# Attention with a dense layer behind it: one softmax for both heads of the 64-row first tile, and a new order of steps

## Chip, cores, metric

One Trainium2 chip, one of its cores. The metric is device time in microseconds (us) of one execution. Engines: PE multiplies matrices, DVE and POOL work elementwise on vectors, ACT applies functions and copies, SP issues most transfers.

## What is computed

```python
B, H, S, D = 4, 8, 576, 64                      # q, k, v: [B, H, S, D]
scores = q @ k.T / sqrt(D), causal              # per head, S x S
a = softmax(scores);  local = a @ v
phi = where(q > 0, q, exp(q) - 1) + 1
mem = (phi @ M_prev) / (phi @ z_prev + 1e-6)
attn = g * mem + (1 - g) * local                # g = sigmoid(beta) of the head
x = attn as [B*S, H*D]                          # [2304, 512]
r = relu(x @ w_in)                              # [2304, 2048]
out = (s * r * r + b) @ w_out                   # [2304, 512]
```

## The kernel before

The 32 heads are taken two at a time, in 16 pairs (`attention(g)`, four pairs for each of the four batch rows). The 576 rows of a head are cut into five tiles of queries: tile 0 with 64 rows, tiles 1 to 4 with 128. Tile 0 is loaded twice, on partitions 0 to 63 and 64 to 127. Buffers of a pair alternate (`u = g % 2`).

For a pair the steps are: load q and k transposed (`load_qk`, L340), q in rows (L291) and z (L292); the feature map of q (`phi`, ACT L295 and L300, DVE L301, products with z L305, normalisers on DVE L307 to L311, writes into P L318); score matmuls on PE in three visits (`scores`, L370 in fp32 for pairs 0 to 7; L364 for pairs 8 to 15, as three fp32r products of a high and a low half that `split` makes, L396 and L398). DVE adds the mask and takes the minimum of each row (`red`, L377), ACT takes the exponential and its sum (`ex`, L383), DVE inverts the sums (L440, L441), POOL or DVE scales the rows (`scale`, L389). PE transposes P in four banks (`bank`, L468), ACT or DVE copies them from PSUM (`copy`, L477 to L484), and `second` (L520) multiplies by V and M. The result is split into a high and a low fp32r half (L541, L542) as `xs`. Weights `w_in` are converted in 20 pieces (`convert`, L564 to L579). The first matrix product (`mm1`, L586 to L588) takes a batch row at a time, in groups of 12 matmuls, two halves of 6 (`first`); what is left of it runs after the attention, with PSUM tiles named hps, beside the preparation of `w_out`. The second product (L866 to L870, yps) is last.

The steps of the attention and the groups of `first` are given to a planner (`Plan.add`) with an engine, a cost and what they read and write. `Plan.deal(ORDER)` puts the steps of each engine in the order of a long table of numbers and merges the engines by modelled starts; so ORDER fixes what stands in a row on every engine, and each engine works through its row in order. `Plan.waits` finds waits of PE in that model and fills them with matmuls of no use (`warm`, L247). Letters choose engines by pair: RELU, ZMUL, PUTS (writes into P), COPY (banks), SCAL (scalings), HIGH and LOW (halves of weights), QL (low halves of q and k); HOME chooses the PSUM pool of a group.

In tile 0 the softmax ran per head on all 128 partitions, so each row was worked twice; the fourth bank (k = 3) took tile 0 from partitions 64 to 127 alone, and had 4 transposes in one PSUM tile and 6 in the other.

## Time and profile before

| | us |
|---|---|
| median of 3 runs (539.62 to 540.48) | 539.95 |
| the profiled execution | 540.74 |
| its span, first to last instruction | 538.9 |
| PE busy in the span | 529.4 |
| ACT busy | 408.1 |
| DVE busy | 406.8 |
| POOL busy | 276.4 |
| first row of the rest of the first product (tile hps) starts at | 270.96 |

The busy time of PE is 98% of the span, and the granted clock is full in every slice. These are sums over stages: in the first tenth of the run ACT and DVE are busy almost without a break, later PE is. So the reader should take each stage by itself.

### The profile page before, as it was taken

The page shows a single profiled execution, that of the slowest core. Times are in us where ns is not written, and L with a number is a line of the kernel's source. Part 1 is how long each engine was busy: PE and PEld are TensorE (multiplying, and loading weights), DVE is VectorE, ACT ScalarE, POOL GpSimd, SP SyncE. Part 2 cuts the span into 40 slices and gives each one's busy share as a digit, 9 for nine tenths or more (in the row PEclk, how much of TensorE's full clock was granted, in tenths as well). Part 3 has the DMA queues.
Part 4 walks back from the last instruction along what each step waited for, and adds up shares of the span by engine and source line. Part 5 has one row for each costly group of instructions (what it writes and reads, how often), then busy time and mean ns, then how long its engine had stood idle before and what let it go on. Part 6 is the DMA issues. An engine that isn't in the chain of part 4 may idle for free.

```text
span 538.9 us, 11602 instructions
## 1 busy us (share of the span) xinstructions
PE 529.4 (98%) x4158; PEld 444.4 (82%) x4158; DVE 406.8 (75%) x986; ACT 408.1 (76%) x898; POOL 276.4 (51%) x275
## 2 busy tenths in 40 slices
PE   8989999999999999999999999999999999999997
PEld 6767777777878778877788888899999998999996
DVE  5999998998877958334169796435798889889873
ACT  6999999889987637547346679769987887897840
POOL 4999557663784623022100001407768768768760
PEclk9999999999999999999999999999999999999999
DMA  7666667755243621121294746356354353452101
GB/s 223 183 178 193 227 219 253 227 155 196 89 150 101 223 84 59 61 79 44 90 376 165 267 174 219 128 192 204 110 161 121 115 167 114 129 174 89 40 30 40
DMA packets 56666, 81.51 MB, mean 151 GB/s; under 512 B 7584, under 2 KB 39072, under 8 KB 56608
## 3 DMA queue, kind: packets, MB, share of 16 engines
q1 hardware_dynamic: 54064, 78.63, 44.8%
q10 hardware_dynamic: 2544, 2.14, 1.2%
q8 instruction: 33, 0.54, 0.4%
q14 instruction: 25, 0.20, 0.1%
HBM read 57.15 MB, written 23.59 MB: 150 GB/s over the span
## 4 chain that ended last, share of the span: by engine, by line
PE 90%; ACT 6%; DVE 2%; issue 1%; DMA 1%; ACTq 0%; DVEq 0%
PE yps L866 12%; PE yps L870 11%; PE sb L520 7%; PE tb L586 7%; PE tb L587 6%; PE tb L588 6%; PE hps L586 5%; PE hps L587 5%; PE hps L588 5%; PE yps L869 5%; PE yps L868 5%; PE tb L468 4%; PE sb L364 4%; ACT P L383 3%; PE sb L370 2%; PE sb L586 1%
## 5 line engine op out<-in xcount | busy, mean ns | idle before, releaser
L389 POOL TENSOR_SCALAR P<-P,sr,omg 128x448 f32<-128x448 f32 (+4 forms) x120 | 89.2, 758 | 37.0 <-DVE sr L441 26.3
L870 PE MATMUL yps<-rb,op 128*128 128x256 f32 x360 | 101.1, 281 | 0.0
L383 ACT ACTIVATE P<-P,mn 128x448 f32<-128x448 f32 (+4 forms) x160 | 90.0, 568 | 9.6 <-DVE mn L377 9.3
L377 DVE CUSTOM_DVE_ANT_0 P<-sb,mask 128x320 f32<-128x320 f32 (+4 forms) x160 | 72.6, 480 | 24.4 <-PE sb L364 21.8
L866 PE MATMUL yps<-rb,op 128*128 128x512 f32 x216 | 76.9, 396 | 0.0
L870 PEld LDWEIGHTS yps<-rb,op 128*128 128x128 f32 x360 | 67.9, 189 | 0.0
L846 POOL TENSOR_TENSOR sum<-src 128x512 f32<-128x512 f32 x10 | 13.0, 1298 | 91.2 <-ACT src L830 76.6
L854 POOL TENSOR_TENSOR op<-src,op 128x512 fp32r<-128x512 f32 x30 | 43.9, 1484 | 20.2 <-ACT op L853 20.1
L877 DVE TENSOR_TENSOR yu<-yu,yps 128x256 f32<-128x256 f32 x90 | 36.5, 414 | 20.0 <-PE yps L870 19.0
L866 PEld LDWEIGHTS yps<-rb,op 128*128 128x128 f32 x216 | 40.6, 188 | 9.0
L468 PEld LDWEIGHTS tb<-ident,P 64*128 64x128 f32 x928 | 35.9, 139 | 9.6 <-issue 4.3
L468 PE MATMUL tb<-ident,P 64*128 64x64 f32 x928 | 40.9, 226 | 2.2 <-DVE xs L542 0.7
L868 PE MATMUL yps<-rb,op 128*128 128x256 f32 x144 | 40.5, 281 | 0.0
L869 PE MATMUL yps<-rb,op 128*128 128x256 f32 x144 | 40.5, 281 | 0.0
L853 ACT CAST op<-src 128x512 fp32r<-128x512 f32 x50 | 30.5, 615 | 12.0 <-PE yps L870 9.6
L854 DVE TENSOR_TENSOR op<-sum,op 128x512 fp32r<-128x512 f32 x36 | 38.7, 1075 | 0.3 <-ACT op L853 0.2
L593 ACT ACTIVATE r<-hps 128x256 f32<-128x256 f32 x62 | 21.8, 385 | 19.4 <-DMA r_d<-r 14.4
L854 POOL TENSOR_TENSOR op<-w1H,op 128x512 fp32r<-128x512 f32 x24 | 35.0, 1489 | 0.0
L318 POOL TENSOR_TENSOR P<-qs,nrm 128x384 f32<-128x384 f32 (+1 forms) x24 | 18.8, 797 | 31.5 <-DVE nrm L311 23.0
L586 PE MATMUL tb<-xs,w0H 128*128 128x512 f32 x80 | 32.9, 412 | 0.0
L383 ACT ACTIVATION_READ_ACCUMULATOR P<-P,mn 128x1 f32 x160 | 32.3, 202 | 0.0
L370 PE MATMUL sb<-qk 64*128 64x288 f32 (+4 forms) x192 | 30.3, 411 | 1.9 <-DVE mn L377 1.7
(177 smaller groups left out, 1618.5 us busy)
## 6 DMA issues: line engine op xcount, KB each, us to landing
r_d<-r SPq DMA_DIRECT2D x41, 256.0 KB, 2.3
src<-r_d SPq DMA_DIRECT2D x20, 512.0 KB, 4.4
qk<-in_qk_t_dram SPq DMA_DIRECT2D x15, 576.0 KB, 5.0
raw<-in_moe_w_out_dram SPq DMA_DIRECT2D x16, 512.0 KB, 6.2
w1H<-r_d SPq DMA_DIRECT2D x16, 512.0 KB, 4.7
xa<-in_moe_w_in_dram SPq DMA_DIRECT2D x12, 512.0 KB, 4.8
r_d<-r SPq DMA_DIRECT2D x48, 128.0 KB, 1.9
qs<-in_q_rows_dram SPq DMA_DIRECT2D x16, 320.0 KB, 3.2
```

The costliest lines, as they stand in the source:

```text
L377: nc.vector.tensor_tensor_reduce(P[:, j, PB[i] + 64:PB[i] + 64 + n], at(ps, j, o, n), m, -SCALE, 3.0e38, ALU.add, ALU.min, mn[:, j, i:i + 1])
L383: nc.scalar.activation(pt, pt, AF.Exp, scale=-1.0, bias=mn[:, j, i:i + 1], accum_out=sm[:, j, i, 0:1])
L389: e.tensor_scalar(pt, pt, sr[:, j, i:i + 1], omg[:, h:h + 1], ALU.mult, ALU.mult)
L468: nc.tensor.transpose(TB[ps[h]][:, o[h]:o[h] + 64], P[rs, j, c:c + 128], ident[rs, rs], tile_position=(64 * h, 0))
L586: nc.tensor.matmul(ps, lhsT=wH[:, p, fs], rhs=xs[:, 0], start=p == 0, stop=False)
L587: nc.tensor.matmul(ps, lhsT=wH[:, p, fs], rhs=xs[:, 1], start=False, stop=False)
L588: nc.tensor.matmul(ps, lhsT=wL[:, p, fs], rhs=xs[:, 0], start=False, stop=p == NP - 1)
L854: (nc.gpsimd if m in ONPOOL else nc.vector).tensor_sub(L, x, H.bitcast(F32))
L866: nc.tensor.matmul(tile, lhsT=H, rhs=B, start=f == 0, stop=False)
L868: nc.tensor.matmul(ps, lhsT=H, rhs=B[:, 0], start=f == 0, stop=False)
L869: nc.tensor.matmul(ps, lhsT=H, rhs=B[:, 1], start=False, stop=False)
L870: nc.tensor.matmul(ps, lhsT=L, rhs=B[:, 0], start=False, stop=f == KF - 1)
```

## The change

For tile 0 the two heads now share one set of 128 partitions: head 0 keeps rows on partitions 0 to 63, head 1 on 64 to 127. `red` stays two instructions of 64 partitions each, writing into one place; `ex` and `scale` are one instruction each. A small write (`put01`) brings head 1's feature map of tile 0 into that place, `open_gates` makes a column of gates (OM) that has head 0's gate above and head 1's below, and the fourth bank has five transposes in each of its PSUM tiles, copied in two pieces. Pairs 8 to 15 score tile 0 in fp32 straight from q and k, so `split` skips the first 128 columns. `Plan.waits` may fill a wait from the time when a PSUM tile comes free in it, and with one matmul too. The letters, modelled costs of transfers, HOME and the table ORDER are new; the counts of steps differ by what is named above.

```diff
@@ Plan.waits
-            n = int((b["start"] - a["end"] - 0.4) / cost)
-            free = [(pool, k) for pool in pools for k, held in enumerate(self.held[pool])
-                    if all(z <= a["end"] or y >= b["start"] for y, z in held)]
-            if n > 1 and free:
-                more.append(dict(start=a["end"], fn=lambda n=n, at=free[0]: fn(n, *at)))
+            free = []
+            for pool in pools:
+                for k, held in enumerate(self.held[pool]):
+                    if all(y >= b["start"] or z < b["start"] for y, z in held):
+                        free.append((max([a["end"]] + [z + self.LAT for y, z in held if a["end"] < z < b["start"]]), pool, k))
...
+            n = int((b["start"] - t - 0.4) / cost)
+            if n > 0:
@@ setup
         warm(WARM, TB[3])
+        nc.tensor.matmul(TB[3][:, :64], lhsT=busy, rhs=busy[:, :64], start=True, stop=True)
@@ letters (PUTS, HIGH and LOW shown of eight)
-    PUTS = "DDPPDPPDPPPPPPPP"
-    HIGH, LOW = "PPAPAAPPAAAAAAAAAAPA", "PDPDDPPDDDPDPDDDDDDD"
+    PUTS = "PDPPDPPDPPPPPDPP"
+    HIGH, LOW = "APAAAAPAAAAAAAAAAAAP", "PDPDDPDPDDPPDDDDDDDD"
@@ phi
+        def put01():
+            put(384, 768, slice(1, None, -1))
+            o = P[64:128, 0, PB[0]:PB[0] + 64]
+            vec.tensor_mul(o, q[64:128, 0, 1], n[64:128, 0, 1].to_broadcast([64, 64]))
@@ scores
-                if fast:
+                if fast and i:
@@ red
+            if i == 0:
+                rs = slice(64 * j, 64 * j + 64)
+                nc.vector.tensor_tensor_reduce(
+                    P[rs, 0, PB[0] + 64:PB[0] + 128], at(ps, j, o, n)[rs], mask[rs, 576:640], -SCALE, 3.0e38, ALU.add, ALU.min, mn[rs, 0, 0:1])
+                return
@@ scale
-            e.tensor_scalar(pt, pt, sr[:, j, i:i + 1], omg[:, h:h + 1], ALU.mult, ALU.mult)
+            e.tensor_scalar(pt, pt, sr[:, j, i:i + 1], omg[:, h:h + 1] if i else OM[:, p:p + 1], ALU.mult, ALU.mult)
@@ split of pairs 8 to 15
-            for k, (a, z) in enumerate(((QF, QF + S), (0, QF))):
+            for k, (a, z) in enumerate(((QF, QF + S), (128, QF))):
@@ the exponentials and the scalings
-                    add("ACT", EXP[i], lambda i=i, j=j: ex(i, j), r + 0.15 + 0.01 * k, [("mn", u, i, j)],
-                        [("p", u, i, j), ("sm", u, i, j)])
+                    if i or j:
+                        add("ACT", EXP[i], lambda i=i, j=j * (i > 0): ex(i, j), r + 0.15 + 0.01 * k, [("mn", u, i, h) for h in ((j,) if i else range(2))],
+                            [("p", u, i, j), ("sm", u, i, j)] + [("p", u, 0, 0), ("sm", u, 0, 0)] * (i == 0))
-                for j in range(2):
+                for j in heads(i):
@@ bank
-            o = [0, 0]
+            o = [64, 64] if k == 3 else [0, 0]
-                        if i == 0 and h == 0:
+                        if i == 0:
+                            if h == j:
+                                nc.tensor.transpose(
+                                    TB[ps[h]][:, 0:64], P[rs, 0, c:c + 128], ident[rs, rs], tile_position=(64 * h, 0))
                             continue
@@ copy, k = 3
-            elif h:
-                put(F[:, :, 0:384].rearrange("p j (r c) -> p j r c", c=128)[:, :, :, 0:64],
-                    t[:, 0:384].rearrange("p (j r c) -> p j r c", j=2, c=64))
             else:
-                put(half(F[:, :, 64:320]), t[:, 0:256].rearrange("p (j r c) -> p j r c", j=2, c=64))
+                put(half(F[:, :, 64:320]), t[:, 64:320].rearrange("p (j r c) -> p j r c", j=2, c=64))
+                put(F[:, h, 0:64], t[:, 0:64])
@@ gates
+    def open_gates():
+        for j in range(2):
+            nc.gpsimd.tensor_copy(OM[64 * j:64 * j + 64], omg.rearrange("r (p j) -> r p j", j=2)[64 * j:64 * j + 64, :, j])
@@ ORDER, first numbers of the table
-        0, 1, 5, 50, 11, 14, 16, 32, 2, 4, 7, 3, 6, 8, 30, 33, 36, 40, 53, 76, 81, 87, 84, 13, 18, 20, 21, 25, 19, 23, 24, 28, 39, 42, 66, 62, 54, 52, 22, 27,
+        0, 3, 5, 95, 13, 19, 21, 27, 29, 1, 4, 9, 2, 6, 7, 22, 26, 35, 40, 55, 63, 72, 90, 79, 12, 17, 18, 30, 15, 38, 23, 36, 42, 43, 51, 54, 62, 16, 24, 32,
```

On ACT, the end of the fourth pair (g = 3; pt and F are the copies of its banks, w0H the rounding of a weight piece, P an exponential). Before:

```order
L477 COPY pt<-tb_100 128x8x64
L477 COPY pt<-tb_101 128x8x64
L479 COPY F_125<-tb_99 128x2x4x64
L479 COPY F_125<-tb_98 128x2x4x64
L484 COPY F_125<-tb_100 128x2x2x64
L481 COPY F_125<-tb_101 128x2x3x64
L566 ACTIVATE xa<-xa 128x256
```

After:

```order
L500 COPY pt<-tb_100 128x8x64
L500 COPY pt<-tb_98 128x8x64
L502 COPY F_126<-tb_101 128x2x4x64
L502 COPY F_126<-tb_99 128x2x4x64
L504 COPY F_126<-tb_100 128x2x2x64
L505 COPY F_126<-tb_100 128x64
L504 COPY F_126<-tb_98 128x2x2x64
L505 COPY F_126<-tb_98 128x64
L401 ACTIVATE P_121,sm_117<-P_121,mn_115 128x192
```

The copies of 128x2x3x64 and 128x2x2x64 became two of 128x2x2x64 and two of 128x64.

On SP, the first transfers of the program (qk_106, qs_110 and z_108 belong to the first pair, qk_107, qs_111 and z_109 to the second). Before:

```order
L340 DMA qk_106<-in_qk_t_dram 128x2x192
L340 DMA qk_106<-in_qk_t_dram 128x2x256
L291 DMA qs_110<-in_q_rows_dram 128x640
L340 DMA qk_106<-in_qk_t_dram 128x2x128
L292 DMA z_108<-in_z_prev_dram 128x128
L340 DMA qk_107<-in_qk_t_dram 128x1152
```

After:

```order
L353 DMA qk_106<-in_qk_t_dram 128x2x192
L353 DMA qk_106<-in_qk_t_dram 128x2x256
L299 DMA qs_110<-in_q_rows_dram 128x640
L300 DMA z_108<-in_z_prev_dram 128x128
L300 DMA z_109<-in_z_prev_dram 128x128
L353 DMA qk_106<-in_qk_t_dram 128x2x128
L353 DMA qk_107<-in_qk_t_dram 128x1152
```

Both z loads moved ahead of the last piece of the first pair's q and k.

On PE, a visit of scores of a pair from 8 on (x6 counts three products for each of two heads). Before:

```order
L364 MATMUL sb_97<-qks 128x448 x6
L364 MATMUL sb_97<-qks 128x64 x6
L364 MATMUL sb_97<-qks 128x320 x6
L364 MATMUL sb_97<-qks 128x192 x6
```

After:

```order
L377 MATMUL sb_96<-qks 128x448 x6
L383 MATMUL sb_96<-qk_106 128x64 x2
L377 MATMUL sb_97<-qks 128x320 x6
L377 MATMUL sb_97<-qks 128x192 x6
```

The six products of 64 columns became two, read from qk.

## Rows read from the trace of the kernel before

**Rows 1.** Windows: length; busy us of PE, PEld, DVE, ACT, POOL; granted clock; DMA

```profile
7.50:53.40 45.90, 42.70 (x492) 31.88 (x490) 44.59 (x173) 45.87 (x136) 41.12 (x55) 1.00 0.66 202
...
56.60:271.00 214.40, 213.51 (x1920) 166.08 (x1917) 153.84 (x472) 160.29 (x421) 102.29 (x118) 1.00 0.43 139
```

**Rows 2.** Waits of PE from 56 to 272: who ended them, us, times, longest

```profile
PE tb L468 <- DVE nrm L311: 0.6, 1, 0.6
PE sb L520 <- DVE mn L377: 0.3, 1, 0.3
```

**Rows 3.** The chain of waits, 0 to 60: start, us, what

```profile
52.67 0.64 ACT F L481
53.36 3.35 PE tb L520 x32
```

**Rows 4.** Timeline of ACT, 38.7 to 53.5: start, us, instruction

```profile
39.46 0.56 ACT L481 COPY F<-tb 128x384 f32<-128x384 f32 x1
39.83 0.46 ACT L484 COPY F<-tb 128x256 f32<-128x256 f32 x1
40.10 0.50 ACT L575 CAST w0H<-xa 128x256 fp32r<-128x256 f32 x1
40.40 0.44 ACT L383 ACTIVATE P<-P,mn 128x64 f32<-128x64 f32 x1
...
40.75 0.64 ACT L383 ACTIVATE P<-P,mn 128x320 f32<-128x320 f32 x1
...
47.63 0.29 ACT L541 CAST x<-tb 128x64 fp32r<-128x64 f32 x1
47.73 0.47 ACT L541 CAST xs<-tb 128x256 fp32r<-128x256 f32 x1
```

**Rows 5.** Groups by shape on DVE, 0 to 53.4: busy us, mean ns

```profile
L318 DVE TENSOR_TENSOR P<-qs,nrm 128x384 f32<-128x384 f32 x2 | 1.3, 648 | 0.0
```

**Rows 6.** Groups by shape on PE, 56 to 271

```profile
L364 PE MATMUL sb<-qks 64*128 64x64 f32 x48 | 3.5, 244 | 0.0
L370 PE MATMUL sb<-qk 64*128 64x64 f32 x8 | 0.7, 244 | 0.0
```

**Rows 7.** Timeline of PE, 52 to 58, the first product's start

```profile
56.64 0.50 PE L586 MATMUL tb<-xs,w0H 128*128 128x512 f32 x1
56.98 0.39 PE L587 MATMUL tb<-xs,w0H 128*128 128x512 f32 x1
57.21 0.39 PE L588 MATMUL tb<-xs,w0L 128*128 128x512 f32 x1
```

**Rows 8.** Transfers issued from 0 to 4: count, size each, us from issue to landing

```profile
qk<-in_qk_t_dram SPq DMA_DIRECT2D x1, 128.0 KB, 4.4
z<-in_z_prev_dram SPq DMA_DIRECT2D x1, 64.0 KB, 5.7
```

**Rows 9.** Timeline of all engines, 0 to 14

```profile
2.74 0.55 SPq L340 DMA_DIRECT2D qk<-in_qk_t_dram  x1
3.34 0.60 SPq L292 DMA_DIRECT2D z<-in_z_prev_dram  x1
...
8.61 1.57 PE L370 MATMUL sb<-qk 64*128 64x288 f32 x8
...
10.21 0.76 DVE L377 CUSTOM_DVE_ANT_0 P<-sb,mask 128x576 f32<-128x576 f32 x1
```

**Rows 10.** Transfers issued from 23 to 25

```profile
xa<-in_moe_w_in_dram SPq DMA_DIRECT2D x1, 256.0 KB, 2.8
z<-in_z_prev_dram SPq DMA_DIRECT2D x1, 64.0 KB, 2.9
```

**Rows 11.** Windows: busy us of each engine, 56 to 80

```profile
56.00:80.00 24.00, 24.00 (x170) 19.02 (x166) 23.60 (x78) 23.57 (x62) 13.11 (x15) 1.00 0.65 212
```

**Rows 12.** Timeline of PE, 65 to 67 and 85 to 90: bursts of scores

```profile
65.03 1.24 PE L370 MATMUL sb<-qk 64*128 64x288 f32 x8
...
85.49 1.48 PE L370 MATMUL sb<-qk 64*128 64x288 f32 x8
```

More of the change, by code (lines that the diff above doesn't have):

```diff
@@ L132, in waits @@
         for a, b in zip(pe, pe[1:]):
-            n = int((b["start"] - a["end"] - 0.4) / cost)
-            free = [(pool, k) for pool in pools for k, held in enumerate(self.held[pool])
-                    if all(z <= a["end"] or y >= b["start"] for y, z in held)]
-            if n > 1 and free:
-                more.append(dict(start=a["end"], fn=lambda n=n, at=free[0]: fn(n, *at)))
+            free = []
[3 more added lines that the diff above has]
+                        free.append((max([a["end"]] + [z + self.LAT for y, z in held if a["end"] < z < b["start"]]), pool, k))
+            if not free:
+                continue
+            t, pool, k = min(free, key=lambda x: x[0])
+            n = int((b["start"] - t - 0.4) / cost)
+            if n > 0:
+                more.append(dict(start=a["end"], fn=lambda n=n, pool=pool, k=k: fn(n, pool, k)))
         return more
@@ L231, in attention_moe_kernel @@
     NRM = two([128, 5, 2, 1], "nrm")
+    OM = ap1.tile([128, NP], F32, name="om")
     MN, SM, SR = two([128, 2, 5], "mn"), two([128, 2, 5, 2], "sm"), two([128, 2, 5], "sr")
@@ L345, in attention @@
         for v, (a, z) in enumerate(chunks):
-            add("SP", 0.9 if a == 0 and g else 0.5, lambda a=a, z=z: load_qk(a, z), (r0 if g else 0) - 4.0 + 0.01 * v, writes=[("qk", u, v)],
-                bytes=128 * 8 * (z - a) + 32768 * (a == 0 and g > 0))
+            add("SP", 0.9 if g else 0.6, lambda a=a, z=z: load_qk(a, z), (r0 if g else 0) - 4.0 + 0.01 * v, writes=[("qk", u, v)],
+                bytes=(400000, 190000, 200000)[v] if g == 0 else 380000 if g == 1 else 128 * 8 * (z - a) + 32768, slack=2 if g else 1)
         if g == 0:
@@ L413, in attention @@
             if fast:
-                cost = sum(n + 32 for _, _, n, _ in group) / 800 + 0.05
+                cost = sum(max(107, (n + 32) / 2.4 + 2) for i, _, n, _ in group if i) * 0.003 + (0.22 if v == 0 else 0.05)
             add("PE", cost, lambda group=group, ps=ps: scores(group, ps), r,
-                [(x, u, k) for x in ("qh", "ql") for k in range(2)] if fast else [("qk", u, k) for k in range((1, 2, 2, 3)[v] if g == 0 else 1)] + [("qk", 0, "d")] * (g == 0),
+                [(x, u, k) for x in ("qh", "ql") for k in range(2)] + [("qk", u, 0)] * (v == 0) if fast else [("qk", u, k) for k in range((1, 2, 2, 3)[v] if g == 0 else 1)] + [("qk", 0, "d")] * (g == 0),
                 [("sc", g, v), "visit"], take=[(ps, "S")] * (2 if v == len(visits) - 1 else 1), mode="row")
@@ L422, in attention @@
                     take=[(free, "T")], give=[(free, 0, "T")], mode="row")
+            heads = lambda i: range(2) if i else range(1)
             tiles = [(i, o - c0) for i, c0, n, o in group if c0 + n == QW[i]]
@@ L434, in attention @@
                 continue
-            keys = [("sm", u, i, j) for i in mine for j in range(2)]
-            inv = [("sr", u, i, j) for i in mine for j in range(2)]
+            keys = [("sm", u, i, j) for i in mine for j in heads(i)]
+            inv = [("sr", u, i, j) for i in mine for j in heads(i)]
             low = sorted(mine)
@@ L492, in attention @@
             PS.update({k: [] for k in ks})
-            add("PE", sum(0.11 + 0.11 * len(BANKS[k]) - (k == 3) * 0.06 for k in ks), lambda ks=ks: [bank(k, PS[k]) for k in ks], r,
+            add("PE", sum(0.11 + 0.11 * len(BANKS[k]) - (k == 3) * 0.12 for k in ks), lambda ks=ks: [bank(k, PS[k]) for k in ks], r,
                 [("p", u, i, j) for i in tiles for j in range(2)] + [("phi", u, i) for k in ks for kt, i in BANKS[k] if kt == 0]
@@ L500, in attention @@
             for h in range(2):
[L501 removed]
+                cost = dict(A=0.48 if k < 3 else 0.36, D=0.58 if k < 3 else 0.45)
                 c = COPY[g][k]
```

32 lines of the change are left out of this document (16 added, 16 removed), and 97 rows, old and new, of the table ORDER.

## The prediction, made before the changed kernel ran

> **What bounds the kernel now.** I read the windows first, then the waits of PE, then the chain of waits, then single rows of ACT and PE. The windows split the run into a head and a body [rows 1]. In the head, 7.5 to 53.4, ACT is busy 45.87 of 45.90 us and DVE 44.59, while PE is busy 42.70 and part of that is warm-up work. From 56.6 to 271.0 PE is busy 213.51 of 214.40 us; ACT (160.29) and DVE (153.84) have room. The last 268 us, from 271.0 on, hold the rest of the first matrix product and the second one, which the diff leaves alone; I take them as unchanged. The waits of PE between 56 and 272 are two, 0.6 us for the normalisers (L311) and 0.3 us for a row minimum (L377) [rows 2]. The chain shows the hand-over: ACT's copy F L481 at 52.67 (the last copy of the fourth pair of heads) releases `second` on PE at 53.36 for 3.35 us, and behind it stands the first product [rows 3]. So the end is: when ACT finishes the fourth pair's last copy, plus PE's work from there. A saving on POOL, or on ACT after 56 us, is worth nothing by itself; one on ACT before 53 us, or on PE after it, is worth its full size.
>
> The sum is made against the profiled execution, 540.74 us with a span of 538.9. The median of the three runs is 539.95, 0.8 lower; what I find as a difference is taken from that median.
>
> **ACT in the head.** I counted in the order what stands on ACT up to that last copy, before and after. Three kinds differ. (a) Exponentials of 64 columns: 9 before, 5 after. One starts at 40.40 and the next instruction at 40.75, so 0.35 each, four of them: -1.4. (b) Copies of the fourth bank: pairs 2 and 3 have theirs on ACT. Before, one of 384 columns (39.46 to 39.83, 0.37) and one of 256 (39.83 to 40.10, 0.27); after, two of 256 and two of 64. The 64-column copy isn't in the trace; its nearest row is the 64-column CAST from PSUM, which gives ACT back after 0.10 (47.63 to 47.73). Per pair 0.74 against 0.64, two pairs: +0.2. Bounds of the small copy are 0.10 and the 0.27 of the 256-column one, so +0.2 to +0.9; I take the low end, since the CAST has its very shape and source. (c) Roundings of weights (w0H, 256 columns): 3 before, 5 after, because two pieces leave POOL. 40.10 to 40.40 is 0.30 each: +0.6. Sum -0.6, all rows of [rows 4]. It stands on the path only if ACT stays as dense as it is now.
>
> [...]
>
> What hides the rest: the minima of the first tile are still two instructions a pair, of 64 partitions now, so DVE is charged nothing for them. DVE gives up the two writes of pair 0's feature map (the larger one 0.65 [rows 5]) to POOL and gets small copies for pairs 0 and 1; the order places about as much work ahead of the fourth pair's end on DVE as before, so I take 0. If DVE became later than ACT, the -0.6 would be gone. POOL loses one 64-column scaling a pair and gains one 64x64 write; it idled 4.8 of 45.9 us in the head [rows 1], which covers that. The two small copies of `open_gates` precede POOL's first real work. Their cost without that cover would be a few tenths.
>
> **PE in the body.** (d) For pairs 8 to 15 the scores of the first tile go back from six short fp32r matmuls to two fp32 ones. Grouped by shape, 48 rows of fp32r 64x64 are busy 3.5 us, 0.44 for each of eight pairs, and 8 rows of fp32 64x64 (each fp32 matmul has two) 0.7 us, 0.35 for each of two pairs [rows 6]. That is 0.09 a pair, -0.7, in a stretch where PE never rests. What a change from fp32r to fp32 inside the burst costs isn't shown; bounds are 0 and 0.11 a pair (the next price), which would eat it. I take 0. (e) PE changes its tiling (scores and transposes, `second`, full products) 79 times before the last stage in the order of before and 76 times after. Entering the full mode costs 0.11: the first L586 to the next at 0.34 (56.64 to 56.98) against 0.23 (56.98 to 57.21) [rows 7]. Three times 0.1: -0.3. (f) The two waits, 0.9 together [rows 2]: both are waits for DVE, and DVE's row around them is rearranged. Bounds 0 and -0.9; nothing tells which, so I take the middle, -0.45. The transposes of the fourth bank are ten a pair both times, and the warm-up matmuls 40 both times, put into other gaps; 0 each, as long as the gaps are real. Where a gap turns out shorter than its fill, the fill delays what stands behind it; without cover all of it would cost at most what the idle part of the head holds for PE, 3.2 us (45.90 less 42.70 [rows 1]), so I keep that out of the sum and leave it to the range.
>
> (g) The half group begun early: in both orders the first product stands right behind the fourth `second`, and the constant EARLY is 1 in both. Nothing for it in the sum.
>
> **SP at the start.** This is the term with a bad end. The changed order issues both z loads ahead of the last piece of the first pair's q and k. Before, that piece was issued at 2.74 and the z load behind it at 3.34 [rows 9]; they landed 4.4 and 5.7 us after their issue [rows 8], so at 7.1 and 9.0: the z load came 1.9 us behind. The scores that need the piece started at 8.61, and their first reader on DVE at 10.21 [rows 9], about 0.8 after the middle of the 1.57 us burst, where the first head's scores are done. Later, a z load takes 2.9 us where the load issued just ahead of it takes 2.8 [rows 10], so it lands about one issue behind, half a microsecond. Two z loads at 0.5 put the piece at 8.1, in time; two at 1.9 put it at 10.9, 2.3 late for PE and 1.5 late for DVE. Bounds 0 and +2.3; I take +0.3, since the later row is the plainer one and the slow load shared the queues with the next pair's. [...]
>
> **Sum:** -0.6 -0.7 -0.3 -0.45 +0.3 = -1.75. From 539.95: 538.2.
>
> **Rivals.** *Only PE's part comes.* The head is held by DVE, which is nearly as dense as ACT (44.59 against 45.87), or the start costs 1.0 to 1.5 us and eats ACT's 0.6; then d and e and perhaps f stay: about -0.3 to -1.0, so 539.0 to 539.7. For it speaks DVE's density; against it that pair 0's writes leave DVE.
>
> *The fifth pair comes too early: slower.* On PE 78 matmuls of the first product stand between the fourth and the fifth `second` before, and 60 after. At 0.23 each [rows 7] PE arrives 4.1 us sooner at copies that ACT must have made, and ACT is dense there, 23.57 of 24.00 us [rows 11]. ACT's own row between the fourth and the fifth pair's last copies shrinks from 47 instructions to 40; at the 0.30 to 0.37 us of [rows 4] that is 2.1 to 2.6 us less, or more where they are wide ones. If ACT isn't ready, PE waits there for up to 4.1: 539.95 - 1.75 + 4.1 = 542.3. It is slower than before once that wait passes 1.75, and measurably so from 2.9. Against it: before, the last of these copies had time to spare, since PE worked through products up to the fifth `second` without any wait in [rows 2].
>
> *More than the waits shown.* The same burst of eight rows of fp32 scores (four matmuls of 288 columns) takes 1.24 us at 65.03 and 1.48 at 85.49 [rows 12]: the two heads may start apart when their buffers come free apart, and no view books that as idle. Seven bursts of fp32 scores stand in the body; if the new order lines up five of them, and takes all of f, another 1.2 + 0.45 go: 536.6.
>
> *It doesn't do what it says*: the early half group (g) doesn't appear; its absence is in the sum already.
>
> **How the numbers follow.** Forecast 538.2, 0.50; only PE's part, 0.25; fifth pair too early, 0.10; more than shown, 0.15. The range takes the forecast's bounds (copies +0.7, f from 0 to -0.9, d's mode price +0.9, the start +2.0, not all at once) and reaches into the rivals on both sides: 536.6 to 540.5. A change under 0.2% (1.1 us) can hardly be told from none: faster is below 538.87. The forecast lies 0.7 below that line, so about four fifths of it counts, with all of the fourth case: 0.57. Within 0.2%: what is left of the forecast and most of the second case, 0.33. Slower: 0.10.
>
> **What would show it.** In the changed kernel's profile the last copy of the fourth pair on ACT should stand about 0.3 us earlier than 52.67, and the fourth `second` near 53.0; the stretch from there to the end of the first products' attention part should be shorter by 1 to 1.5 us; the last piece of the first pair should land before 9 us. I am wrong if ACT has idle time in the head, if the first scores' last group starts after 9.5, or if PE shows new waits of a microsecond after 56 us, first of all at the fifth `second`.

## The result, and the profile after

The changed kernel is slower: 543.62 us median of 4 runs (543.30 to 545.09) against 540.22 of the kernel before, ratio 1.0059 with a 95% interval of 1.0045 to 1.0073. Forecast was 538.2, so it missed by 5.4 us and in sign. The profiled execution after is the one of 545.09 us (span 543.3); before it was 540.74 (span 538.9).

The marks I read in each trace are the starts of `second` for the first four pairs, of the last `second`, and of the first product of the last stage (hps). All in us from the span's start:

| kernel | `second` 1, 2, 3, 4 | last `second` | hps | end | body | hand-over |
|---|---|---|---|---|---|---|
| before | 22.03, 32.96, 43.61, 53.36 | 267.67 | 270.96 | 538.95 | 214.31 | 3.29 |
| changed | 23.65, 36.65, 47.74, 57.89 | 270.21 | 275.31 | 543.27 | 212.32 | 5.10 |

Body is from the fourth to the last `second`, hand-over from there to hps. From hps to the end it is 267.99 before and 267.95 after: the last stage is what it was. So 4.5 us were lost in the head (53.36 to 57.89), 1.8 at the hand-over, and 2.0 gained in the body.

Windows of the changed kernel over head and body answer to [rows 1]: length; busy us of PE, PEld, DVE, ACT, POOL; granted clock; share and rate of DMA.

```profile
7.50:57.90 50.40, 44.49 (x493) 33.36 (x491) 47.61 (x184) 46.54 (x139) 40.05 (x55) 0.97 0.57 183
61.30:275.30 214.00, 211.57 (x1901) 164.62 (x1901) 159.05 (x492) 157.93 (x417) 86.07 (x107) 1.00 0.43 137
```

In the head ACT does 0.7 us more than before, and now it rests for 3.9 us. DVE is busy 3.0 us longer. The granted clock, full before, is 0.97. So the engine that the prediction called dense is no longer dense throughout the head.

Waits of PE from 56 to 277 answer to [rows 2]: who ended them; us, times, longest.

```profile
PE hps L607 <- DVE xs L563: 1.7, 1, 1.7
PE sb L383 <- DVE mn L395: 0.4, 1, 0.4
PE tb L488 <- DVE P L333: 0.2, 1, 0.2
```

The first is the hand-over. Timeline of ACT there: start, us, instruction, idle time before it and what ended it.

```profile
273.61 0.21 ACT L562 CAST x<-sb 128x64 fp32r<-128x64 f32 x1 [4.55 <-PE sb L541]
273.72 0.59 ACT L562 CAST xs<-sb 128x512 fp32r<-128x512 f32 x1
274.20 0.62 ACT L630 ACTIVATE r<-sb 128x512 f32<-128x512 f32 x1
```

The last row is the ReLU of the last product that was begun before the last `second`. Its matmuls were over by 270.3; it waits in ACT's row behind the casts of the last pair, and they wait for `second`. In the kernel before, ACT's row has it ahead of those casts:

```profile
267.83 0.60 ACT L609 ACTIVATE r<-sb 128x512 f32<-128x512 f32 x1 [0.55 <-ACT F L479]
...
271.18 0.59 ACT L541 CAST xs<-sb 128x512 fp32r<-128x512 f32 x1
```

The chain of waits in the head, which answers to [rows 3], runs over DVE, not ACT, from 21.7 to 32 us, and mostly over ACT from 34.9 on. At the place of interest, start, us, what:

```profile
27.47 0.68 DVE qs L309
28.15 0.34 DVE P L326
28.52 1.44 DVE P L333
```

L333 is the new write of 64x64 elements for the second pair. Timeline of DVE and, below it, of POOL at that place:

```profile
28.07 0.42 DVE L326 TENSOR_TENSOR P<-qs,nrm 128x256 f32<-128x256 f32 x1
28.52 1.44 DVE L333 TENSOR_TENSOR P<-qs,nrm 64x64 f32<-64x64 f32 x1
29.99 0.23 DVE L563 TENSOR_TENSOR x<-tb,x 128x64 fp32r<-128x64 f32 x1
```

```profile
28.24 1.65 POOL L313 TENSOR_TENSOR phr<-qs,z 128x640 f32<-128x640 f32 x1 [0.86 <-DVE qs L309]
```

POOL's product begins at 28.24, while the first of DVE's two writes runs, and ends at 29.89. DVE's second write ends at 29.96.

The clock in that stretch, in windows of 3 us (columns as above):

```profile
24.00:27.00 3.00, 3.00 (x32) 1.85 (x28) 2.97 (x16) 2.97 (x9) 2.89 (x5) 1.00 0.15 19
27.00:30.00 3.00, 2.00 (x26) 1.76 (x24) 2.90 (x7) 2.27 (x11) 2.14 (x3) 1.00 0.24 86
30.00:33.00 3.00, 2.05 (x12) 1.25 (x14) 3.00 (x8) 1.89 (x5) 1.83 (x4) 0.68 0.11 9
33.00:36.00 3.00, 2.91 (x49) 2.70 (x47) 1.66 (x9) 2.08 (x5) 1.89 (x4) 0.75 0.80 232
```

DVE has hardly any idle time from 24 to 33; ACT, POOL and the transfers have much. PE waits for a third of 27 to 33, and then the granted clock goes to 0.68 and 0.75: the trace lists it as 0.50 from 31.08 to 34.49 us and as 1.00 on either side of that.

### The profile page after: what moved, and what is told of

Its sections match the earlier page's. It is cut to its first block, busy times and chain, and to the rows that moved or that the text cites. A ratio compares the mean times of both kernels' runs of the same rounds, so it can differ in the third digit from the quotient of the medians.

```text
span 543.3 us, 11585 instructions
## 1 busy us (share of the span) xinstructions
PE 530.3 (98%) x4144; PEld 446.7 (82%) x4144; DVE 408.8 (75%) x1007; ACT 405.6 (75%) x890; POOL 258.5 (48%) x264
## 4 chain that ended last, share of the span: by engine, by line
PE 86%; DVE 6%; ACT 4%; issue 2%; DMA 1%; POOL 1%; SPq 0%; DVEq 0%
PE yps L892 12%; PE yps L896 11%; PE sb L541 7%; PE hps L607 5%; PE hps L608 5%; PE hps L609 5%; PE tb L607 5%; PE yps L895 5%; PE yps L894 5%; PE tb L609 5%; PE tb L608 5%; PE tb L491 4%; PE sb L377 4%; PE sb L607 2%; PE sb L383 2%; PE sb L609 2%
## 5 line engine op out<-in xcount | busy, mean ns | idle before, releaser
L401 ACT ACTIVATE P<-P,mn 128x320 f32<-128x320 f32 (+4 forms) x144 | 84.3, 592 | 10.2 <-DVE mn L395 10.2
L395 DVE CUSTOM_DVE_ANT_0 P<-sb,mask 128x192 f32<-128x192 f32 (+3 forms) x128 | 67.8, 549 | 18.5 <-PE sb L377 10.7
L407 POOL TENSOR_SCALAR P<-P,sr,omg 128x448 f32<-128x448 f32 (+3 forms) x86 | 63.7, 751 | 28.8 <-DVE sr L461 16.2
L491 PE MATMUL tb<-ident,P 64*128 64x64 f32 x896 | 39.7, 228 | 1.8 <-POOL P L407 1.6
L383 PE MATMUL sb<-qk 64*128 64x64 f32 (+4 forms) x224 | 33.8, 407 | 3.4 <-DVE mn L395 3.4
L880 DVE TENSOR_TENSOR op<-sum,op 128x512 fp32r<-128x512 f32 x36 | 35.5, 989 | 0.3 <-ACT op L879 0.2
L880 POOL TENSOR_TENSOR op<-w1H,op 128x512 fp32r<-128x512 f32 x24 | 34.9, 1482 | 0.0
L500 ACT COPY pt<-tb 128x512 f32<-128x512 f32 x52 | 29.1, 592 | 6.3 <-PE tb L491 6.3
L607 PE MATMUL tb<-xs,w0H 128*128 128x512 f32 x76 | 31.2, 411 | 0.0
L326 POOL TENSOR_TENSOR P<-qs,nrm 128x256 f32<-128x256 f32 (+1 forms) x24 | 18.6, 785 | 26.4 <-PE tb L491 19.3
```

The costliest lines, as they stand in the source:

```text
L395: nc.vector.tensor_tensor_reduce(P[:, j, PB[i] + 64:PB[i] + 64 + n], at(ps, j, o, n), m, -SCALE, 3.0e38, ALU.add, ALU.min, mn[:, j, i:i + 1])
L401: nc.scalar.activation(pt, pt, AF.Exp, scale=-1.0, bias=mn[:, j, i:i + 1], accum_out=sm[:, j, i, 0:1])
L407: e.tensor_scalar(pt, pt, sr[:, j, i:i + 1], omg[:, h:h + 1] if i else OM[:, p:p + 1], ALU.mult, ALU.mult)
L491: nc.tensor.transpose(TB[ps[h]][:, o[h]:o[h] + 64], P[rs, j, c:c + 128], ident[rs, rs], tile_position=(64 * h, 0))
L607: nc.tensor.matmul(ps, lhsT=wH[:, p, fs], rhs=xs[:, 0], start=p == 0, stop=False)
L880: (nc.gpsimd if m in ONPOOL else nc.vector).tensor_sub(L, x, H.bitcast(F32))
```

## Experiments

Theory after the two traces: three separate losses (hand-over; the small write on DVE; the start), and a gain in the body, 2.0 where the sum had 1.45 for (d), (e) and (f). Rivals are named with each. The marks of all runs are in one table behind the experiments.

### The hand-over: which buffer, and what stands in ACT's row

`hand_after` and `hand_before` exchange the two score buffers:

```diff
     TB = [ps_a.tile([128, 512], F32, name=f"tb{k}") for k in range(4)]
+    SB.reverse()
```

`hand2_after` does so too, and in ORDER puts the ReLU of the last product ahead of the last pair's casts, its store with it. ACT's row there:

```diff
+ACTIVATE r<-sb 128x512
 CAST x<-sb 128x64
 CAST xs<-sb 128x512
-ACTIVATE r<-sb 128x512
```

> The changed kernel with the two score buffers (the SB tiles) exchanged throughout; nothing else. Theory: in the changed kernel the last `second` lies in the buffer whose PSUM the first product of the last stage (hps) takes over, so that product waits for the last casts: its trace has a wait of 1.75 us there, and 5.10 us from the last `second` to that product against 3.29 before. Exchanged, the wait is gone, that stretch is back at 3.3 us and the median falls by 1.8 us, from 543.6 to about 541.8. Rival: the wait stands for casts that come late whatever the buffer (ACT and DVE behind); then the stretch stays near 5 us and the time within 0.3 us of 543.6.

> The kernel before with the two score buffers exchanged; nothing else. Theory (the place of the last `second` makes the wait): a wait of 1.7 us for the casts appears at the first product of the last stage, and the time rises by 1.8 us, from 540.2 to about 542.0. Rival (casts are late only in the changed kernel): no wait, time within 0.3 us of 540.2.

> The changed kernel with the score buffers exchanged (as in hand_after) and, on ACT, the ReLU of the last product of the attention part put ahead of the casts of the last pair, where it stands in the kernel before (its store on SP with it). Theory: two things hold both score buffers until after the last `second`: one holds its result until the casts are done, the other holds that product until the ReLU, which the changed order puts behind the casts. Only with both undone can hps begin at once: the stretch from the last `second` to hps goes to 3.3 us (5.1 in the changed kernel, 4.66 with the exchange alone), everything behind it is as long as ever (267.95 us), so 1.8 us less than the changed kernel. Rival: something else is late there too, and the stretch stays above 4 us.

Measured: `hand_after` 543.73 us, ratio to before 1.0054 (1.0041 to 1.0066), hand-over 4.66. `hand_before` 543.05, ratio 1.0045 (1.0027 to 1.0062), hand-over 5.10. `hand2_after` 542.06, ratio 1.0035 (1.0022 to 1.0047), hand-over 3.29. Waits of PE at the hand-over, `hand_after` and then `hand_before`; in `hand2_after` there is none:

```profile
PE hps L608 <- ACT r L631: 1.3, 1, 1.3
```

```profile
PE hps L587 <- DVE xs L543: 1.8, 1, 1.8
```

Timeline of `hand2_after`, all engines:

```profile
270.52 0.60 ACT L631 ACTIVATE r<-sb 128x512 f32<-128x512 f32 x1 [1.29 <-issue]
...
273.65 0.50 PE L608 MATMUL hps<-xs,w1H 128*128 128x512 f32 x1
...
273.87 0.59 ACT L563 CAST xs<-sb 128x512 fp32r<-128x512 f32 x1
```

My first expectation was wrong: the exchange alone gave 0.45, not 1.8. It showed the second cause: with the last `second` out of the way, hps waits for the ReLU, since the other buffer is held by that product. With both undone the wait is gone and hps starts before the casts. `hand_before` shows the first cause by itself: where the last `second` lies in the buffer that hps takes over, the wait appears in the old kernel too. Its median rose by 2.6 instead of 1.8; its runs spread over 3 us, and what makes up the other 0.8 is open. The hand-over costs the changed kernel 1.8 us.

### The small write of the second pair

`put_after` takes the 64x64 write off DVE for this pair; `first_after` keeps it there and changes the order of the two writes.

```diff
 # put_after, in put01
-            vec.tensor_mul(o, q[64:128, 0, 1], n[64:128, 0, 1].to_broadcast([64, 64]))
+            if g == 1:
+                nc.scalar.activation(o, q[64:128, 0, 1], AF.Copy, scale=n[64:128, 0, 1])
+            else:
+                vec.tensor_mul(o, q[64:128, 0, 1], n[64:128, 0, 1].to_broadcast([64, 64]))
 # first_after, in put01, for g == 1
-            put(384, 768, slice(1, None, -1))
             vec.tensor_mul(o, q[64:128, 0, 1], n[64:128, 0, 1].to_broadcast([64, 64]))
+            put(384, 768, slice(1, None, -1))
```

> The changed kernel with one instruction moved: the 64x64 write of the second pair's feature map (L333, for pair 1 only) goes from DVE to ACT, which idles there. Theory: on DVE that write took 1.45 us, because POOL's long product (L313, 1.65 us) began in the gap between the two writes and DVE's write ended only when POOL's product did (where nothing runs on POOL the same write takes 0.22); DVE has no idle time there, so 1.2 us is lost between the first and the second `second`. Moved, the distance of these two falls from 11.75 us (without a lower clock) to about 10.6, and the time by about 1.2 us. Rival: DVE isn't what PE waits for; the distance stays at 11.7 and the time too.

> The changed kernel with the two writes of the second pair's first tiles on DVE in the other order: the 64x64 one first, then the one of 256 columns. It asks what made the 64x64 write take 1.45 us. Theory (POOL's turn): whichever of the two comes second falls behind POOL's product, since POOL begins in the gap between them; the 64x64 write takes 0.2 and the 256-column one 1.5 to 1.7 instead of 0.42, and the time stays that of the changed kernel. Rival (the shape, 64 partitions from the 64th on): the 64x64 write stays at 1.2 us or more wherever it stands.

Measured: `put_after` 542.77, ratio 1.0050 (1.0030 to 1.0070); from the first to the second `second` 10.83 us. `first_after` 543.80, ratio 1.0062 (1.0047 to 1.0077). Timeline of DVE in `first_after`:

```profile
27.37 0.22 DVE L333 TENSOR_TENSOR P<-qs,nrm 64x64 f32<-64x64 f32 x1
27.63 1.65 DVE L326 TENSOR_TENSOR P<-qs,nrm 128x256 f32<-128x256 f32 x1
29.31 0.22 DVE L566 TENSOR_TENSOR x<-tb,x 128x64 fp32r<-128x64 f32 x1
```

and of POOL:

```profile
27.43 1.57 POOL L313 TENSOR_TENSOR phr<-qs,z 128x640 f32<-128x640 f32 x1 [0.86 <-DVE qs L309]
```

Now the 64x64 write takes 0.22 and the wide one 1.65 instead of 0.42. So it isn't the shape: whichever write comes second is the long one, and it ends with POOL's product, at 27.63 + 1.65 = 29.28 against 27.43 + 1.57 = 29.00 here, at 29.96 against 29.89 in the changed kernel. POOL's product begins while the first of the two writes runs, both times, and not in the gap between them. Where POOL runs nothing, the changed kernel has the two writes of a later pair at 0.42 and 0.22 us, the 64x64 one second:

```profile
113.38 0.42 DVE L326 TENSOR_TENSOR P<-qs,nrm 128x256 f32<-128x256 f32 x1
113.84 0.22 DVE L333 TENSOR_TENSOR P<-qs,nrm 64x64 f32<-64x64 f32 x1
```

That the second write waits for POOL is read from these ends; by what means it is held, no run shows.

What it costs is 0.92 us in these marks (11.75 to 10.83). That is the upper end: in `all_after` below, with the write on ACT too, the first `second` comes 0.59 earlier than in `put_after`, but the next one only 0.09 earlier (34.30 against 34.39), and the distance is 11.33, so 0.4 less than 11.75. In none of the 7 runs of `put_after` was the span's mean clock below 0.999. Windows of `put_after`, as those of the changed kernel above:

```profile
27.00:30.00 3.00, 2.54 (x28) 2.12 (x30) 2.94 (x10) 2.63 (x12) 2.14 (x3) 1.00 0.24 80
30.00:33.00 3.00, 2.44 (x48) 1.85 (x46) 2.80 (x11) 3.00 (x8) 3.00 (x6) 1.00 0.45 125
33.00:36.00 3.00, 2.85 (x32) 2.55 (x30) 2.60 (x13) 3.00 (x8) 2.01 (x4) 1.00 0.93 295
```

PE is busy for 4.98 us from 27 to 33 instead of 4.05, and the granted clock is 1.00. Over all runs, those that have the changed order with this write on DVE show a mean clock of 0.997 or less in 17 of 44 executions, those with the write on ACT in none of 77 (most of these have other parts undone too).

### Once more the changed kernel, and its first steps

`after_again` is the changed kernel. `start_after` changes positions in ORDER (DVE's row shown; on ACT's queue gin's load goes ahead of that of q and k, and on SP both z loads behind the last q and k piece of the first pair):

```diff
+L666 TENSOR_SCALAR gin<-gin 128x8
+L672 RECIPROCAL omg<-gin 128x8
+L391 minimum 64x64, head 0
 L395 minimum 128x192, head 0
-L391 minimum 64x64, head 0
 L391 minimum 64x64, head 1
-L666 TENSOR_SCALAR gin<-gin 128x8
-L672 RECIPROCAL omg<-gin 128x8
 L395 minimum 128x192, head 1
```

> The changed kernel itself, to read its trace once more beside the others: 543.6 us; the wait of 1.75 us at the hand-over and the start of the third group of scores near 7.9 us should be there again. What is between the first and the second `second` (13.0 us, 10.9 before) is the question: a theory of lateness in the order makes it the same again, a disturbance of that one execution makes it shorter.

> The changed kernel with the first steps in the places that they had before: the load of gin ahead of the one of q and k on ACT's queue, the two short steps on gin (L666, L672) ahead of the first minima on DVE, the 64-row tile's minimum ahead of the 192-row one's, and both z loads behind the last q and k piece of the first pair on SP. Theory: these cost 1.3 us at the third group of scores (7.93 against 6.57 us) and everything after is late by it; undone, the third group starts near 6.6, the first `second` near 22.3 instead of 23.65, the fourth about 1.3 us earlier than now, and the median falls from 543.6 to about 542.3. Rival: the head is held elsewhere (between the first and the second pair PE loses another 2 us), and an earlier start only makes the later waits longer: time within 0.4 us of 543.6.

Measured: `after_again` 544.96, ratio 1.0082 (1.0069 to 1.0096); `start_after` 543.32, ratio 1.0054 (1.0040 to 1.0068). The question on the second pair has a mixed answer: the distance from the first `second` to the next is 12.52 in `after_again` and 13.00 in the first profile, both with a lowered clock, and 11.74 or 11.75 in `hand_after`, `start_after` and `fp32r_after`, where the clock stayed up. So 11.75 is what the order itself gives (10.93 before), and the clock adds 0.8 to 1.3 to this distance where it falls, which it did in some executions only. Part of that can come back: `after_again` and `first_after` are 0.5 and 0.3 faster from the second to the third `second`, so by the third the price is 0.3 to 1.3. The gain of `start_after` against two medians 1.3 apart told nothing; the last experiment settles it.

### The scores in fp32, from both sides

`fp32r_after` undoes this part in the changed kernel, `fp32_before` does it alone in the kernel before (there the loads of q and k of pairs 13 and 15 stand a few steps later in ORDER).

```diff
 # fp32r_after (fp32_before: the reverse of the first edit)
-                if fast and i:
+                if fast:
-            for k, (a, z) in enumerate(((QF, QF + S), (128, QF))):
+            for k, (a, z) in enumerate(((QF, QF + S), (0, QF))):
```

> The changed kernel with the first tile's scores of pairs 8 to 15 back in fp32r (six short matmuls for two, and the rounding of 128 more columns of q and k). It undoes one part of the change alone. Theory: that part saves PE what the sum says, 0.1 us a pair; undone, the 448- and 64-column group goes back from 0.85 to 0.96 us, the body gets 0.7 to 0.8 us longer and so does the time. Rival: the body's gain of 2.0 us comes from the waits and mode changes alone, and the time stays within 0.2 us.

> The kernel before with one part of the change alone: the first tile's scores of pairs 8 to 15 in fp32 (two matmuls for six); two loads of later pairs' q and k are issued a few steps later, since these scores still read the old ones. Theory: the part is worth 1.08 us, as its undoing in the changed kernel cost (body 213.39 against 212.30); body 214.3 to 213.2, time 540.45 to 539.4, and nothing in the head changes. Rival: in the order of before PE waits there for others (it had 0.9 us of waits), and what the matmuls save goes into longer waits: within 0.3 us of 540.4.

Measured: `fp32r_after` 544.81, ratio 1.0082 (1.0067 to 1.0097), body 213.39 against 212.32. `fp32_before` 539.51, ratio 0.9981 (0.9971 to 0.9991): this one beats both kernels. Its body is 212.33. The body of the profiled execution before (214.31) has the 0.9 us of waits of [rows 2]; `hand_before`, the same order, has none and 213.31. Against that, `fp32_before` gains 0.98, and `fp32r_after` loses 1.07, of which 0.2 is a wait for a minimum that the changed kernel doesn't have: the part is worth about 1.0 us.

### All three undone, and then two more

`all_after` is `hand2_after`, `put_after` and `start_after` together. On that base `pool0_after` puts the first pair's two writes back on DVE, next to each other, with its 64x64 write on ACT, and `high_after` puts three roundings back on POOL:

```diff
 # pool0_after
-    PUTS = "PDPPDPPDPPPPPDPP"
+    PUTS = "DDPPDPPDPPPPPDPP"
 # high_after (HIGH)
-    "APAAAAPAAAAAAAAAAAAP"
+    "PPAPAAPPAAAAAAAAAAAP"
```

> The changed kernel with all three undone: score buffers exchanged and the ReLU ahead of the casts (as in hand2_after), the second pair's 64x64 write on ACT (as in put_after), the first steps in the places they had before (as in start_after). Theory: the three losses add: -1.8, -1.2 and -0.4 us, so 3.4 less than the changed kernel, about even with the kernel before (540.4) or a little under it, since the body's gain of 2 us is kept. Rival: they overlap (a wait takes the place of the one removed), and the time stays above 541.5.

> all_after with one thing more undone: the writes of the first pair's feature map back on DVE, as before the change, both in one place; its 64x64 write on ACT. Theory: the changed kernel puts three writes of 2.6 us on POOL (0.61, 0.98 for the 64x64 one, 0.83) ahead of the two scalings of 576 columns that the first pair's last transposes wait for, and POOL is the one that is late there: the transposes stand at 20.1 us against 19.16 before, the first `second` 0.94 later. Undone, the first `second` comes at 22.2 to 22.4 (22.97 in all_after with the clock up from the start, 22.03 before) and the time falls by 0.6. Rival: DVE, which gets 1.0 us of work, is as late as POOL was; the first `second` stays near 23 and the time too.

> all_after with three roundings of weights (the pieces 0, 3 and 7, L594) back on POOL, as before the change. Theory: what is still lost in the head, 0.43 and 0.42 us between the second, third and fourth `second` (11.08 and 10.17 against 10.65 and 9.75), is ACT, which has no idle time there and 0.65 us more work in each; three roundings of 0.3 us off it give 0.6 to 0.9 back, and the time falls by about 0.7. POOL, which idles 11 us of the head in the changed kernel, takes them for nothing. Rival: DVE, dense there too, holds PE; the distances stay at 11.1 and 10.2.

Measured: `all_after` 541.07, ratio 1.0007 (0.9998 to 1.0016), so it is even with the kernel before. Whether the losses add in full is less clear: 541.07 is 2.6 and 3.9 below the two medians of the changed kernel, but among executions with the clock up the spans fall by 2.3 only (541.4 to 542.0 against 538.7 to 539.5), since the small write gives back 0.4 here and not 0.92. `pool0_after` 540.95, ratio 1.0002 (0.9994 to 1.0011): no gain. `high_after` 540.45, ratio 0.9999 (0.9991 to 1.0008): 0.5 less than `pool0_after` on the same chip, 0.6 less than `all_after` on another, with intervals that overlap.

In `pool0_after` POOL was free earlier, but the two scalings of 576 columns waited for DVE, which has the writes now; the first row is `pool0_after`, the second, in a fence of its own, `all_after`:

```profile
17.73 2.16 POOL L411 TENSOR_SCALAR P<-P,sr,omg 128x576 f32<-128x576 f32 x2 [1.74 <-DVE sr L465]
```

```profile
18.35 1.63 POOL L411 TENSOR_SCALAR P<-P,sr,omg 128x576 f32<-128x576 f32 x2
```

They end at 19.89 and 19.98. The rival was right: work moved from POOL to DVE moves the wait.

`high_after` gained what I expected, 0.63 us, but from the first to the second `second` (11.33 to 10.70), not where I placed it. The distances I wanted to explain stayed at 11.09 and, a little longer, 10.39 (10.17), so up to the fourth `second` 0.40 is left of the 0.63. The second of the two distances isn't a loss: `hand_before` and `fp32_before` have 10.35 and 10.36 in the old order, where the profiled execution has 9.75 and then the 0.9 us of waits. The 0.43 from the second to the third `second` (11.08 against 10.65) stay open.

### The first steps, priced

All on the base of `high_after`: `first_steps` takes ORDER's first steps from the changed kernel (the diff of `start_after` reversed), `z_loads` only the two z loads on SP, `high_again` is the base once more. SP's row in `z_loads`:

```diff
+z (pair 0)
+z (pair 1)
 q and k, last piece of pair 0
-z (pair 0)
 q and k, pair 1
 q rows, pair 1
-z (pair 1)
```

> high_after (the changed kernel with hand-over, second pair's 64x64 write and roundings undone), but with the first steps as the changed kernel has them: gin's load second on ACT's queue, its two short steps between the first minima on DVE, the 192-row minimum ahead of the 64-row one, both z loads ahead of the last q and k piece. Theory: these cost 0.4 us in start_after against the changed kernel (third group of scores 7.51 against 7.93 where the first matmuls ran slowly in both); so the time is 0.4 above high_after's 540.45, or more where the clock is up early. Rival: the first stretch differs by more than that between executions of one kernel (third group at 6.57 to 8.06 us), and the median shows nothing: within 0.2 us of high_after.

> high_after with only the two z loads of the first pairs put ahead of the last q and k piece on SP, as in the changed kernel: the term of the sum that was set at +0.3 between 0 and +2.3. Theory now: that piece landed in time in every run (5.4 us after its issue at 3.7 is 9.1, while PE's last group of scores began at 9.4 and later), so the two loads cost nothing: within 0.2 us of high_after. Rival: +0.3 as the sum had it, or more.

> high_after itself, as the measure for the two others on the same chip: 540.45 us, even with the kernel before.

Measured: `first_steps` 540.88, ratio 1.0003 (0.9994 to 1.0013); `z_loads` 540.24, ratio 0.9995 (0.9986 to 1.0004); `high_again` 540.68, ratio 0.9999 (0.9991 to 1.0008). The z loads cost nothing that shows. `first_steps` is 0.2 above `high_again` and 0.6 above `z_loads` on the same chip, with intervals that overlap: the other first steps cost a few tenths at most, and which of them isn't shown.

The first stretch differs between executions of one kernel. First scores and third group of scores on PE, `high_after`:

```profile
4.68 2.51 PE L387 MATMUL sb<-qk 64*128 64x64 f32 x12
7.51 1.02 PE L387 MATMUL sb<-qk 64*128 64x448 f32 x4 [0.31 <-DVE mn L399]
```

and `high_again`, the same kernel:

```profile
4.68 1.42 PE L387 MATMUL sb<-qk 64*128 64x64 f32 x12
6.95 1.02 PE L387 MATMUL sb<-qk 64*128 64x448 f32 x4 [0.84 <-DVE mn L399]
```

The same twelve matmuls take 2.51 or 1.42 us, and 0.6 of it is left at the end (539.0 and 538.4 us span). The traces list the granted clock only from a first entry on, at 7.17 us in `high_after` and 4.85 in `high_again`; ahead of it the windows print 1.00 because nothing is listed, not because full speed was read. The last four of the twelve take 0.74 us each ahead of that entry and 0.43 behind it; they take 0.74 in the changed kernel too (entry at 7.19) and 0.45 in the kernel before (entry at 4.18). That PE's clock was lower ahead of the entry is an estimate from these times; no entry says so. Of the first profile's 1.36 us at this group (7.93 against 6.57) some 0.6 are this, not the order.

### The marks of all runs

| kernel | 1st `second` | to 2nd | to 3rd | to 4th | body | hand-over | span | mean clock |
|---|---|---|---|---|---|---|---|---|
| before | 22.03 | 10.93 | 10.65 | 9.75 | 214.31 | 3.29 | 538.9 | 1.000 |
| changed | 23.65 | 13.00 | 11.09 | 10.15 | 212.32 | 5.10 | 543.3 | 0.997 |
| after_again | 22.94 | 12.52 | 10.60 | 10.16 | 212.33 | 5.10 | 541.6 | 0.996 |
| hand_after | 23.02 | 11.75 | 11.08 | 10.16 | 212.25 | 4.66 | 540.9 | 1.000 |
| hand2_after | 23.79 | 13.07 | 11.09 | 10.15 | 212.26 | 3.29 | 541.6 | 0.997 |
| hand_before | 22.09 | 10.90 | 10.65 | 10.35 | 213.31 | 5.10 | 540.3 | 1.000 |
| put_after | 23.56 | 10.83 | 11.08 | 10.17 | 212.30 | 5.10 | 541.0 | 1.000 |
| first_after | 22.85 | 12.59 | 10.81 | 10.14 | 212.31 | 5.10 | 541.8 | 0.995 |
| start_after | 23.23 | 11.74 | 11.09 | 10.15 | 212.32 | 5.10 | 541.6 | 1.000 |
| fp32r_after | 23.16 | 11.74 | 11.10 | 10.17 | 213.39 | 5.10 | 542.6 | 1.000 |
| fp32_before | 23.93 | 10.90 | 10.65 | 10.36 | 212.33 | 3.29 | 539.4 | 1.000 |
| all_after | 22.97 | 11.33 | 11.08 | 10.17 | 212.30 | 3.28 | 539.1 | 0.999 |
| pool0_after | 23.36 | 10.99 | 11.09 | 10.15 | 212.28 | 3.28 | 539.1 | 0.999 |
| high_after | 23.22 | 10.70 | 11.09 | 10.39 | 212.39 | 3.28 | 539.0 | 1.000 |
| first_steps | 23.71 | 10.48 | 11.08 | 10.41 | 212.35 | 3.28 | 539.3 | 0.999 |
| z_loads | 22.70 | 10.71 | 11.09 | 10.39 | 212.40 | 3.29 | 538.6 | 0.999 |
| high_again | 22.66 | 10.70 | 11.09 | 10.40 | 212.32 | 3.29 | 538.4 | 0.999 |

The profile of `fp32_before` is its slowest execution (541.24 of 538.81 to 541.24), with the first clock entry at 10.54 us; its late first `second` is not typical, the body is what it is read for.

First `second` can be compared where the first clock entry comes equally early (4.2 to 4.6 us): 22.03 and 22.09 in the order of before, 22.85 to 23.02 in the changed order (`first_after`, `after_again`, `hand_after`). The order itself costs 0.9 there. With the first steps undone it is 22.66 and 22.70 (`high_again`, `z_loads`, entries at 4.9), so 0.6 of it stays.

## Why the prediction was wrong, step by step

**The hand-over wasn't looked at.** The failed step is "The last 268 us ... I take them as unchanged." They are unchanged, to 0.04 us; but what stands between the last `second` and them is 1.8 us longer. The prediction compared the rows inside head and body and took the border for fixed. The order of the changed kernel has the ReLU behind the casts, so this could have been read from ACT's row alone. Shown by `hand2_after`. The prediction looked for a new wait of a microsecond "first of all at the fifth `second`"; it came here.

**DVE was charged 0, with POOL's idle time as the cover.** The prediction asked of the small write only whether POOL had room for its time. It takes 0.22 us by itself on DVE, but as the second of two writes it took 1.44, up to the end of POOL's product. That is 0.4 to 0.9 on the path (shown by `all_after` and `put_after`), and it left PE short of work. Where the clock then fell, another 0.3 to 1.3 went; that the clock stays up with the write on ACT is shown by the count of executions, that the idle time of PE is the reason is only argued from the windows, and `hand_after` speaks against it as the whole reason.

**"It stands on the path only if ACT stays as dense as it is now."** It did not: ACT rests for 3.9 us in the head. The condition was named, and its failure got 0.25 as *Only PE's part comes*, with DVE as the holder; but the case had no price for DVE being later than ACT.

**(a) and (b), exponentials and copies.** The small copy was priced right. Timeline of ACT in the changed kernel, at the place of [rows 4]:

```profile
57.01 0.44 ACT L504 COPY F<-tb 128x256 f32<-128x256 f32 x1
57.28 0.29 ACT L505 COPY F<-tb 128x64 f32<-128x64 f32 x1
57.38 0.46 ACT L504 COPY F<-tb 128x256 f32<-128x256 f32 x1
57.64 0.31 ACT L505 COPY F<-tb 128x64 f32<-128x64 f32 x1
```

It gives ACT back after 0.10 us (57.28 to 57.38), as the CAST row said. But where DVE holds the path, from 21.7 to 32 us, a saving on ACT is worth nothing. What (a) saved by itself no run shows.

**(c) The roundings were set too high.** +0.6 for two more of them; three taken off ACT gave 0.63 back up to the second `second` in `high_after` and 0.40 up to the fourth, so two are worth 0.3 to 0.4.

**(d) was mis-sized:** -0.7 predicted from the busy time of single matmuls, -1.0 measured. Timeline of PE at a group of 448 and 64 columns with transposes behind it, before and then in the changed kernel:

```profile
156.06 1.12 PE L364 MATMUL sb<-qks 64*128 64x448 f32 x12
157.02 0.71 PE L468 MATMUL tb<-ident,P 64*128 64x64 f32 x16
```

```profile
161.15 0.88 PE L377 MATMUL sb<-qks 64*128 64x448 f32 x6
161.86 0.33 PE L383 MATMUL sb<-qk 64*128 64x64 f32 x4
162.03 0.66 PE L491 MATMUL tb<-ident,P 64*128 64x64 f32 x16
```

From its start to the next instruction the group took 0.96 us and now takes 0.85 to 0.88. Eight such differences are 0.6 to 0.9, so the price of a change from fp32r to fp32 that was feared doesn't show; where the rest of the 1.0 comes from stays open.

**(e) can't be seen by itself:** -0.3 predicted for three mode changes fewer; `fp32_before` with the old order has a body of 212.33 and the changed kernel 212.32. But the changed kernel has two waits for DVE in it, 0.4 and 0.2, and `fp32_before` none, so a gain of up to 0.6 may stand against them. The net of (e) and (f) is nothing.

**(f) was nothing that the change could take:** the 0.9 us of waits are in the profiled execution of before and in no other trace of its order. Where they are missing, the fourth `second` is 0.6 later. Half of 0.9 was counted as a gain that no row of another execution bears out.

**SP at the start: 0, the better bound.** Transfers of the changed kernel issued from 3.6 to 4.3 and, among them, the z load issued at 3.23, answer to [rows 8]: size, us to landing.

```profile
qk<-in_qk_t_dram SPq DMA_DIRECT2D x1, 128.0 KB, 4.4
z<-in_z_prev_dram SPq DMA_DIRECT2D x1, 64.0 KB, 3.7
```

The piece issued at 3.70 landed at 8.1, in time for scores that began at 9.97. It is the case of "two z loads at 0.5"; `z_loads` confirms it. That the first scores' last group began after 9.5 us, which the prediction named as a sign of being wrong, goes with the late first clock entry of that execution: where the entry comes at 4.2 to 4.6 us, the group begins at 9.16 to 9.36 (`first_after`, `after_again`, `hand_after`). The other first steps weren't in the sum; they are a few tenths at most.

**The rivals.** *The fifth pair comes too early* did not come: no wait over 0.4 in the body. *More than the waits shown* didn't either: beyond (d) the body is no shorter than that of `fp32_before`. *Slower* had 0.10 for one mechanism; neither the hand-over, nor the small write, nor the later first `second` was on the list.

**Sum, with the clock up.** The changed kernel's executions with the clock up have spans near 541.5, those of before 538.0 to 539.8 (median 538.6), so about 2.9 is to be explained. The marks give 0.9 (first `second`) + 1.1 (from there to the fourth, 32.98 in `start_after` against 31.90 in `hand_before`) - 1.0 (body, against `hand_before`) + 1.8 (hand-over) = 2.8. The hand-over and the body have an experiment each. Of the 1.1, the small write and the roundings give back 0.8 together (32.18 in `high_after`); their 0.92 and 0.63, each read from one distance, don't add. Open are 0.3 of the 1.1, of the size of the 0.43 between the second and third `second`, and 0.6 of the 0.9 ahead of the first. So `high_after` is even with the kernel before because the 1.0 gained in the body covers 0.9 that is still lost in the head.

## What to carry to other kernels

When an order is new, read the rows across every border between stages: which result still holds the buffer that the next stage takes first, and what stands ahead of the instruction that frees it. A small instruction on DVE isn't priced by its own time alone: here one of 0.22 us took 1.44 beside a product of two tensors on POOL (1.65 us), so ask what POOL runs at that time. And a wait in one profiled execution is no saving before a second trace of the same kernel shows it too.

## What the runs showed that I had not expected

Of two writes on DVE, 0.22 us (64x64) and 0.42 us (128x256) where POOL runs nothing, whichever came second took 1.44 or 1.65 beside a product on POOL of 1.65 or 1.57. The first twelve matmuls after the warm-up took 2.51 or 1.42 us in two executions of one kernel. They took 2.51 in the changed kernel too, while its windows print a granted clock of 1.00 there; the slow ones stand ahead of the first clock entry, where the 1.00 is no reading. And after PE's waits from 27 to 33 the granted clock went to 0.68 and 0.75 in the changed kernel, yet stayed at 1.00 in `hand_after`, where PE waits there no less (busy for 1.38 of 3 us from 27 to 30 and 2.41 of 3 from 30 to 33). In these 6 us PE is idle for 1.95 us in the changed kernel and for 2.21 in `hand_after`. So about as much idle time went with 0.3 to 1.3 us more in one execution and with nothing in another; what decides it stays open.
